# Which tiles are asked for when: three skipped loads and two halved scalings ahead of a mixture of experts

## The chip, the cores and the metric

The kernel runs on one core of a Trainium2 chip. The time is device time in microseconds (us), the median of three runs. TensorE (PE) multiplies; VectorE (DVE), ScalarE (ACT) and GpSimd (POOL) work on tiles in on-chip memory; SyncE (SP) issues nearly all direct transfers, in the order of its instruction queue, and POOL issues the indirect ones.

## What is computed

```python
# q, k, v: (8 batches, 8 heads, 576 positions, 64), float32
scores = q @ k.T / sqrt(64)
ret = scores * Dmat                  # gamma_h ** (i - j) for i >= j, else 0
x = (ret @ v) reshaped to (4608 tokens, 512)
g = argmax(x @ w_group)              # 4 groups, weight g_w = softmax
e = argmax(x @ w_expert[g])          # 4 experts in each, weight e_w = softmax
out[token] = g_w * e_w * (relu(x @ w1[g, e]) @ w2[g, e])      # w1 512x1024, w2 1024x512
```

## The kernel before

The program has two stages. The attention stage goes over 36 tiles of 128 tokens in one Python loop, `for t in range(NT + 1)`. The expert stage then goes over 16 experts, largest group first; the first expert's rows are cut in two passes, and the early one starts while the last attention tiles are still being finished.

Each attention tile has two inputs: `a` (queries and keys, 512 KB) and `b` (keys and values in another layout, 512 KB; every ninth tile needs only the values, 256 KB). They live in two rings of `RB = 7` buffers each, `r1` and `r2`. The weights of the experts use the same two rings: a piece `r` of `w1` (512 KB) takes a buffer of `r1`, a piece of `w2` (512 KB) one of `r2`. Four pieces of each make one expert.

Iteration t of the loop issues, on TensorE in this order: `av(t-1)` (masked scores times values, into `px`), `state(t)` (keys times scaled values, into `pst`), `inter(t-1)` (queries times the running state, into `px`), `scores(t+1)` (into `pss`), and then the transposes `pxt` and the small gate matmuls of earlier tiles. `scale(t+1)` stands ahead of them: it multiplies the values of the next tile by a factor for each head, as eight ScalarE instructions that read `b` and write `vs`. ScalarE then copies the state out of PSUM (`st<-pst`). On ScalarE the eight scalings of tile t+1 stand ahead of the copy of state t, and `state(t+1)` may not write `pst` before that copy has read it. VectorE masks the scores (`sT<-pss`) and scales the output (`xT<-px`). The order of the instructions on each engine is that of the program (a manual schedule on TensorE, `pin` on the others).

Loads run six tiles ahead: iteration t asks for tile t+6 (`loads(t + LOADS - 1, ...)`). From tile 8 on they are "paced": the DMA instruction also waits for the TensorE instruction just ahead of it in the program (`follow`). So in iteration 29 the last tile, 35, is asked for. The first expert is picked in iteration 28 (`pick(0)`, `expert_of(0)`: SP loads its number into a register). In iteration 29 its padding rows are written to the scratch tensor `xs` in DRAM, and `xload(0)` reads its 224 rows back as four transfers `xb`; on SP these wait until the scatters to `xs` that stand ahead of them have landed. The first expert's four weight pieces follow, one for `w1` and one for `w2` in each of the iterations 30 to 33 (`load_piece(r - 7)`). Weights of the second expert are asked for behind the loop.

Of the kernel before, what the change touches and what calls it, by code (L numbers as in the profile page):

```python
# [12 lines left out]
ALU = mybir.AluOpType  # L13
AX = mybir.AxisListType

P = 128
RG = 3
B, H, S, D = 8, 8, 576, 64
# [15 lines left out]
LOADS = 7  # L34
WARM = 8

FULL = 8
PACED = 8
NS = N + P
NT = N // P  # L40
NPIECE = 4
# [30 lines left out]
def moe_retention(ctx, tc, qk, kv, wgt, w1, w2, c_f, out):  # L72
# [7 lines left out]

    xs = dp.tile([E * NS, Q * WQ], F32, name="xs")

    cf = cp.tile([P, KC], F32, name="cf")
    gk = cf[:, KC_GK : KC_GK + 5 * H].rearrange("p (c h) -> p c h", c=5)
# [46 lines left out]
    dve, act, pool, sp = [Ordered(e_) for e_ in (nc.vector, nc.scalar, nc.gpsimd, nc.sync)]  # L131
# [3 lines left out]
    def follow(inst):  # L135

        tc.add_manual_dep(
            inst.ins, recent["pe"].ins.name,
            mybir.DependencyInfo(mybir.DependencyClass.Sync, mybir.DependencyReason.DATA),
            reason="loads apart in time",  # L140
        )
# [10 lines left out]
    def wload(e, pc, part):  # L152
        shape = [P, NKC, 2 * P] if part == 0 else [P, 2, DM]
        r = wp.tile(shape, F32, name=f"r{part + 1}_{e}_{pc}", tag=f"r{part + 1}", bufs=RB)
        w = (w1, w2)[part][bass.ds(ereg[e], 1), pc]
        sp.dma_start(r.rearrange("p c f -> p (c f)"), w.rearrange("o p x -> (o p) x"))
        return r
# [11 lines left out]
    def load_piece(i, parts=(0, 1)):  # L169
        if i < len(pieces):  # L170
            raws.setdefault(i, []).extend(wload(*pieces[i], part) for part in parts)
# [60 lines left out]
    def width_of(p):  # L232

        wide[p] = nc.values_load(
            sizes[0:1, p : p + 1], engines=[mybir.EngineType.PE], min_val=0, max_val=NS,
            skip_runtime_bounds_check_because="a count of rows, compared only",
# [46 lines left out]
    def xpad(p):  # L283

        apart("xs", pool.indirect_dma_start(
            out=xs, out_offset=bass.IndirectOffsetOnAxis(ap=pads[:, p % E : p % E + 1] if p else pad0, axis=0),
            in_=zero, in_offset=None, bounds_check=E * NS - 1, oob_is_err=False,
        ))
# [11 lines left out]
    def pad(rows, e, n, cap):  # L300

        pd = sm.tile([P, 2], F32, name=f"pd_{rows.name}", tag="pd")
        dve.tensor_scalar(pd[:, 0:1], sln[:, 0:1], n, None, ALU.add)
        dve.tensor_scalar(pd[:, 1:2], pd[:, 0:1], float(cap), float(E * NS), ALU.is_ge, ALU.mult)
        dve.tensor_tensor(pd[:, 0:1], pd[:, 0:1], pd[:, 1:2], ALU.add)
        dve.scalar_tensor_tensor(rows, e, float(NS), pd[:, 0:1], ALU.mult, ALU.add)

# [52 lines left out]
    tiles = []  # L360
    for bp in range(B // 2):
        for j in range(9):
            if j < 8:
                b, c = 2 * bp + j // 4, j % 4
# [79 lines left out]
    def xnat_store(t):  # L444
# [5 lines left out]
            out=xs, out_offset=bass.IndirectOffsetOnAxis(ap=g_["sl"][:, r : r + 1], axis=0),  # L450
            in_=xt.rearrange("p q w -> p (q w)"), in_offset=None, bounds_check=E * NS - 1, oob_is_err=False,
        ))
# [83 lines left out]
    def places_pe(t):  # L536

        n = RG
        ob = obs[-1]
        of = ob[:, 1:, :]  # L540
        pp = ps_sm.tile([P, n, E], F32, name=f"pp_{t}", tag="sm")

        def of_all(a):
            return a.unsqueeze(1).to_broadcast([P, n, E])

        pe.matmul(pp, up, of, start=True, stop=False)
        for r in range(1, n):
            pe.matmul(pp[:, r:, :], ones, ob[:, 1 : n - r + 1, :], start=False, stop=False)
        pe.matmul(pp, ones, of_all(ob[:, 0, :]), start=False, stop=False)
        pe.matmul(pp, ones, of_all(ensb), start=False, stop=True)  # L550
        tiles[t]["pp"] = pp
# [61 lines left out]
    def without():  # L613
        dve.tensor_scalar(mia[:, 0], slb, picked["c0"], float(BIG), ALU.is_ge, ALU.mult)
# [74 lines left out]
    with ExitStack() as ac:  # L689
# [7 lines left out]
        def loads(t, nms, paced=False):  # L697
            if t >= NT:
                return
            T = tiles[t]  # L700
            for nm in nms:

                T[nm] = wp.tile([P, 2, DM], F32, name=f"{nm}_{t}", tag=dict(a="r1", b="r2")[nm], bufs=RB)
                if T["m"] and nm == "b":
                    i_ = sp.dma_start(T[nm][:, 1], src[nm][t, :, 1])
                elif t:
                    i_ = sp.dma_start(T[nm], src[nm][t])
                if paced:
                    follow(i_)
            if t == 0 and nms == "b":  # L710

                for nm, i in (("b", 1), ("a", 0), ("a", 1), ("b", 0)):
                    sp.dma_start(T[nm][:, i], src[nm][t, :, i])
            if nms == "a":
                T["qT"], T["kT"] = [T["a"][:, i].rearrange("p (i j) -> p i j", i=NP) for i in range(2)]
            else:
                T["k"], T["v"] = [T["b"][:, i].rearrange("p (h d) -> p h d", h=H) for i in range(2)]
# [21 lines left out]
        def first_gq():  # L739

            dve.memset(gqs[0][:, :, 0:1], D**-0.5)
            for k in range(7):
                w = 2**k
                dve.tensor_tensor(
                    gqs[0][:, :, w : 2 * w], gqs[0][:, :, 0:w],
                    g2[:, :, k].unsqueeze(2).to_broadcast([P, 4, w]), ALU.mult,
                )
# [45 lines left out]
        def scale(t):  # L793

            T = tiles[t]
            T["vs"] = ap.tile([P, H, D], F32, name=f"vs_{t}", tag="vs", bufs=3)
            for h in range(H):
                act.activation(
                    T["vs"][:, h, :], T["v"][:, h, :], AF.Copy, scale=gk[:, T["c"], h : h + 1]
                )  # L800

        def scores(t):

# [111 lines left out]
        def group_end(t, lag):  # L915
            return t - lag + (t - lag + 1 == NT - RG - 1)

        scale(0)
        first_gq()
        scores(0)  # L920
        masked(0)
        for t in range(NT + 1):
            now = t < NT
            paced = t >= PACED
            if not paced:
                loads(t + LOADS - 1, "a")
            r = t - PICK

            choice = choose(group_end(t, 4)) if due(t, 4) else iter(())
            for _ in choice:  # L930
                if t >= NT - RG:
                    break
            if now and due(t, 5):
                places(group_end(t, 5))
            if r == 8:
                without()
            if t + 1 < NT:
                scale(t + 1)
            if t == NT:
                xnat_pe(NT - 6, ps_st)  # L940
            if t:
                av(t - 1)
            if t == NT - 1:
                second = pick(1)
                next(second)
            if not paced:
                loads(t + LOADS - 1, "b")
            if now:
                state(t)
            if paced:  # L950
                loads(t + LOADS - 1, "a", True)
            if t == NT:
                places_pe(NT - RG - 1)
            if t:
                inter(t - 1)
                if t == NT:
                    turned(t - 1)
                    places(NT - RG - 1)
                else:
                    turned(t - 1)  # L960
                    for _ in choice:
                        pass
            if r == 6:
                taken()
                close()
            if due(t, 4):
                weigh(group_end(t, 4))
            if t == NT - 1:
                next(second)
            if t + 1 < NT:  # L970
                scores(t + 1)
                masked(t + 1)
            late_consts(t)
            if now and 6 <= t:
                xnat_pe(t - 6)
                if paced:
                    loads(t + LOADS - 1, "b", True)
                xnat_out(t - 6)
            if now and due(t, 2):
                logits(group_end(t, 2))  # L980
            if due(t, 3):
                gate_pe(group_end(t, 3))
            if now and last_of_group(t - 4):
                places_pe(t - 4)

            u = t - 6
            while 0 <= u and "sl" in tiles[tiles[u]["grp"][-1]] and not tiles[u].get("out"):
                tiles[u]["out"] = True
                u -= 1
            for u in range(max(u + 1, 0), t - 5):  # L990
                if now:
                    xnat_store(u)
            if r == 5:
                for _ in pick(0):
                    pass
                expert_of(0)


            if r == 6:
                xload(0)  # L1000
            if 7 <= r <= 10:
                load_piece(r - 7)
            if r == 9:
                xturn(0, 0, 2)
                xturn(0, 1, 2)
                ids(0)
# [606 lines left out]
```

## Time and profile before

| | |
|---|---|
| median of 3 runs | 564.41 us (563.77 to 566.07) |
| profiled execution | 563.58 us, its span 561.8 us |
| TensorE busy | 547.5 us, 97% of the span |
| VectorE, ScalarE, GpSimd busy | 426.5, 328.0, 259.8 us |
| moved by DMA | 141.93 MB, mean 253 GB/s |
| granted TensorE clock | 0.999 of full speed |

The span runs from the first to the last instruction; the execution's own time is 1.8 us longer. The attention stage takes the first 142 us, and the expert stage the rest. A busy engine is not one at its peak, but with TensorE at 97% only gaps in its row, or work taken off it, can move the time by much. All times of the trace below are counted from the start of the span.

### The profile page before, as it was taken

The page shows a single profiled execution, that of the slowest core. Times are in us where ns is not written, and L with a number is a line of the kernel's source. Part 1 is how long each engine was busy: PE and PEld are TensorE (multiplying, and loading weights), DVE is VectorE, ACT ScalarE, POOL GpSimd, SP SyncE. Part 2 cuts the span into 40 slices and gives each one's busy share as a digit, 9 for nine tenths or more (in the row PEclk, how much of TensorE's full clock was granted, in tenths as well). Part 3 has the DMA queues.
Part 4 walks back from the last instruction along what each step waited for, and adds up shares of the span by engine and source line. Part 5 has one row for each costly group of instructions (what it writes and reads, how often), then busy time and mean ns, then how long its engine had stood idle before and what let it go on. Part 6 is the DMA issues. An engine that isn't in the chain of part 4 may idle for free. (4 is left out here: it accounts for less than half of the span.)

```text
span 561.8 us, 16944 instructions
## 1 busy us (share of the span) xinstructions
PE 547.5 (97%) x6137; PEld 522.7 (93%) x6137; DVE 426.5 (76%) x996; ACT 328.0 (58%) x855; POOL 259.8 (46%) x372
## 2 busy tenths in 40 slices
PE   7999989999999999999999999999999999999995
PEld 4888878878899999999999999999999999999995
DVE  5887768888789768976768596877778678787784
ACT  5687868877646545454555454555546555555554
POOL 0022423233504347464655628374665635638535
PEclk9999999999999999999999999999999999999999
DMA  8999999979784693847475674938475692865671
GB/s 329 416 414 338 342 357 326 371 269 367 268 264 178 179 345 89 324 115 286 128 282 167 244 242 164 325 112 329 120 281 185 239 341 73 331 193 208 227 287 47
DMA packets 61978, 141.93 MB, mean 253 GB/s; under 512 B 9164, under 2 KB 29780, under 8 KB 61872
## 3 DMA queue, kind: packets, MB, share of 16 engines
q1 hardware_dynamic: 52560, 120.32, 60.5%
q0 software_dynamic: 9168, 20.10, 9.4%
q8 instruction: 73, 1.20, 0.9%
q14 instruction: 33, 0.27, 0.1%
q10 hardware_dynamic: 144, 0.05, 0.0%
HBM read 120.08 MB, written 24.68 MB: 258 GB/s over the span
## 5 line engine op out<-in xcount | busy, mean ns | idle before, releaser
L125 POOL DMA_INDIRECT out<-y,ii x155 | 169.2, 1092 | 66.7 <-issue 30.9
L125 DVE TENSOR_TENSOR wl<-r,wh 128x512 fp32r<-128x512 f32 x268 | 172.2, 684 | 2.9
L125 ACT ACTIVATE hh<-ph 128x352 fp32r<-128x352 f32 (+16 forms) x128 | 53.6, 419 | 184.2 <-PE ph L651 136.5
L125 ACT CAST wh<-r 128x512 fp32r<-128x512 f32 x268 | 151.3, 618 | 0.0
L651 PE MATMUL ph<-xTh_m,wh 128*128 128x316 f32 (+12 forms) x504 | 147.2, 292 | 0.5 <-ACT xTh_m L125 0.5
L651 PE MATMUL ph<-xTl_m,wh 128*128 128x316 f32 (+12 forms) x504 | 146.9, 292 | 0.1
L651 PE MATMUL ph<-xTh_m,wl 128*128 128x316 f32 (+12 forms) x504 | 147.0, 292 | 0.0
L1103 PE MATMUL py<-hl,wh 128*128 128x316 f32 (+11 forms) x504 | 147.0, 292 | 0.0
L1101 PE MATMUL py<-hh,wh 128*128 128x316 f32 (+12 forms) x504 | 146.7, 291 | 0.0
L1102 PE MATMUL py<-hh,wl 128*128 128x316 f32 (+11 forms) x504 | 146.7, 291 | 0.0
L125 DVE SCALAR_TENSOR_TENSOR hl<-ph,hh 128x352 fp32r<-128x352 f32 (+15 forms) x126 | 58.2, 462 | 88.1 <-ACT hh L125 87.6
L651 PEld LDWEIGHTS ph<-xTh_m,wh 128*128 128x128 f32 x504 | 95.0, 189 | 0.6 <-ACT xTh_m L125 0.6
L651 PEld LDWEIGHTS ph<-xTl_m,wh 128*128 128x128 f32 x504 | 95.0, 188 | 0.4 <-DVE xTl_m L125 0.4
L1103 PEld LDWEIGHTS py<-hl,wh 128*128 128x128 f32 x504 | 95.0, 188 | 0.0
L651 PEld LDWEIGHTS ph<-xTh_m,wl 128*128 128x128 f32 x504 | 95.0, 189 | 0.0
L1102 PEld LDWEIGHTS py<-hh,wl 128*128 128x128 f32 x504 | 95.0, 188 | 0.0
L1101 PEld LDWEIGHTS py<-hh,wh 128*128 128x128 f32 x504 | 95.0, 188 | 0.0
L125 POOL COPY pace<-hh 1x1 f32<-1x1 f32 x118 | 29.9, 254 | 117.2 <-ACT hh L125 116.8
L125 POOL DMA_INDIRECT xs<-xt,sl x33 | 32.8, 995 | 96.9 <-DVE xT L125 39.5
L125 ACT ACTIVATE vs<-b,cf 128x64 f32<-128x64 f32 x288 | 72.4, 336 | 6.6 <-DMA b<-in_kv 5.5
L125 DVE TENSOR_TENSOR sT<-pss,masks 128x512 f32<-128x512 f32 x72 | 46.0, 680 | 10.1 <-PE pss L811 5.9
L867 PE MATMUL px<-sT,vs 128*64 128x128 f32 x576 | 39.4, 279 | 0.4 <-DVE xT L125 0.3
(187 smaller groups left out, 581.6 us busy)
## 6 DMA issues: line engine op xcount, KB each, us to landing
r<-in_w SPq DMA_DIRECT2D x138, 512.0 KB, 8.2
a<-in_qk SPq DMA_DIRECT2D x35, 512.0 KB, 6.2
b<-in_kv SPq DMA_DIRECT2D x31, 512.0 KB, 7.2
xb<-xs SPq DMA_DIRECT2D x20, 165.0 KB, 3.7
xb<-xs SPq DMA_DIRECT2D x20, 148.5 KB, 3.0
xb<-xs SPq DMA_DIRECT2D x16, 181.5 KB, 4.2
out<-y,ii POOLq DMA_INDIRECT x155, 3.4
b<-in_kv SPq DMA_DIRECT2D x6, 256.0 KB, 4.0
```

What stands on the lines that cost most here:

```text
L125: i_ = f(*a, **k)
L651: pe.matmul(ph[:, :wn], a[:, kc, cs], b[:, kc, x0 : x0 + wn], start=n == 0, stop=n == 3 * NKC - 1)
L867: recent["pe"] = pe.matmul(px[g * D : g * D + D, o, s * P : s * P + P], T["vs"][:, 4 * s + 2 * g + o, :], T["sT"][:, o, 2 * s + g, :], sta ...
L1101: pe.matmul(py[:, :w0], wh[:, f % 2, ds_], hh[:, :w0], start=st_, stop=False)
L1102: pe.matmul(py[:, :w], wl[:, f % 2, ds_], hh[:, :w], start=False, stop=False)
L1103: pe.matmul(py[:, :w], wh[:, f % 2, ds_], hl[:, :w], start=False, stop=sp_)
```

## The change

Three edits. First, iterations 12, 18 and 24 ask for no tile, and every later iteration asks for a nearer one: `ahead(t)` is t+6 up to tile 11, t+5 from 13, t+4 from 19 and t+3 from 25, so that tile 35 is asked for in iteration 32 and not 29. Second, the first expert's weight pieces come one iteration later and in halves, over the iterations 31 to 36. Third, for tiles 1 and 2 ScalarE scales four heads and VectorE the other four, in one instruction (`scale_rest`).

```diff
+SKIP = (12, 18, 24)
...
-            for h in range(H):
+            for h in range(H // 2 if t in (1, 2) else H):
...
+        def scale_rest(t):
+            T = tiles[t]
+            n = H // 2
+            dve.tensor_tensor(
+                T["vs"][:, n:], T["v"][:, n:],
+                gk[:, T["c"], n:].unsqueeze(2).to_broadcast([P, H - n, D]), ALU.mult,
+            )
...
+        def ahead(t):
+            return NT if t in SKIP else t + LOADS - 1 - sum(t > x_ for x_ in SKIP)
...
-                loads(t + LOADS - 1, "a", True)
+                loads(ahead(t), "a", True)
...
+            if t == 0:
+                scale_rest(1)
             if t:
                 inter(t - 1)
...
+            if t == 1:
+                scale_rest(2)
...
-                    loads(t + LOADS - 1, "b", True)
+                    loads(ahead(t), "b", True)
...
-            if 7 <= r <= 10:
-                load_piece(r - 7)
+            for i, part in {8: [(0, 0)], 9: [(1, 0)], 10: [(0, 1), (1, 1)], 11: [(2, 0), (2, 1)],
+                            12: [(3, 0)], 13: [(3, 1)]}.get(r, []):
+                load_piece(i, (part,))
```

No instruction is added to TensorE, POOL or SP, and their rows keep their order, except on SP. There the queue around iteration 29 read, before the change (`a_35` is the queries and keys of tile 35, `xb` the first expert's rows, `r1_0_0` the first piece of its `w1`, `r2_0_0` of its `w2`; `ISA` is register work; the repeated register loads and three more `xb` are left out):

```order
L125 DMA a_34_2415<-in_qk 128x1024
L125 DMA b_34_2443<-in_kv 128x1024
L250 TENSOR_LOAD e0i_71
...
L125 DMA a_35_2512<-in_qk 128x1024
L125 DMA b_35_2563<-in_kv 128x512
L125 ISA
L125 DMA xb_0_2575<-xs_63 32x7x132
...
L125 DMA r1_0_0_2673<-in_w1 128x1024
L125 ISA
L125 DMA r2_0_0_2675<-in_w2 128x1024
```

And after the change:

```order
L126 DMA b_32_2545<-in_kv 128x1024
L126 ISA
L126 DMA xb_0_2557<-xs_63 32x7x132
...
L126 DMA a_33_2604<-in_qk 128x1024
L126 DMA b_33_2648<-in_kv 128x1024
L126 DMA a_34_2695<-in_qk 128x1024
L126 DMA b_34_2731<-in_kv 128x1024
L126 ISA
L126 DMA r1_0_0_2749<-in_w1 128x1024
L126 DMA a_35_2779<-in_qk 128x1024
L126 DMA b_35_2806<-in_kv 128x512
L126 ISA
L126 DMA r1_0_1_2819<-in_w1 128x1024
```

The inputs of tiles 33, 34 and 35, which stood ahead of the four `xb` transfers, now stand behind them, and behind the wait that the first of these has.

On VectorE the start of the program gains two instructions, each between the masked scores of one tile and of the next (after the change):

```order
L126 TENSOR_TENSOR sT_0_195<-pss_110,masks_114 128x512 x2
L126 TENSOR_TENSOR vs_1_200<-b_1_140,cf_64 128x256
L126 TENSOR_TENSOR sT_1_227<-pss_110,masks_114 128x512 x2
L126 TENSOR_TENSOR xT_0_258<-px_0_237,gq0_115 128x4x128
L126 TENSOR_TENSOR vs_2_232<-b_2_144,cf_64 128x256
L126 TENSOR_TENSOR sT_2_269<-pss_110,masks_114 128x512 x2
```

Before, the two rows with `vs` were not there, and ScalarE's queue held eight scalings for each of these tiles where it now holds four.

## Rows read from the trace of the kernel before

**Rows 1.** The page's first part: busy time, share of the span, instructions.

```profile
PE 547.5 (97%) x6137; PEld 522.7 (93%) x6137; DVE 426.5 (76%) x996; ACT 328.0 (58%) x855; POOL 259.8 (46%) x372
```

**Rows 2.** Timeline of TensorE, 40 to 82: start, time, instruction, idle before it.

```profile
43.90 0.34 PE L852 MATMUL pst<-vs,b 128*64 128x64 f32 x4 [1.18 <-issue]
...
71.60 0.49 PE L412 MATMUL pxt<-cf,xT 128*128 128x128 f32 x3 [0.76 <-issue]
...
77.91 0.69 PE L852 MATMUL pst<-vs,b 128*64 128x64 f32 x16 [0.98 <-ACT xt L125]
```

**Rows 3.** Timeline of TensorE at the start, same columns.

```profile
11.32 0.69 PE L852 MATMUL pst<-vs,b 128*64 128x64 f32 x16 [0.66 <-ACT st L125]
...
19.39 1.09 PE L867 MATMUL px<-sT,vs 128*64 128x128 f32 x16
20.31 0.64 PE L852 MATMUL pst<-vs,b 128*64 128x64 f32 x16
```

**Rows 4.** Timeline of ScalarE at the start.

```profile
9.00 2.02 ACT L125 ACTIVATE vs<-b,cf 128x64 f32<-128x64 f32 x8 [3.25 <-DMA b<-in_kv]
10.92 0.35 ACT L125 COPY st<-pst 128x256 f32<-128x256 f32 x1
11.51 2.02 ACT L125 ACTIVATE vs<-b,cf 128x64 f32<-128x64 f32 x8 [0.24 <-DMA b<-in_kv]
...
17.88 2.02 ACT L125 ACTIVATE vs<-b,cf 128x64 f32<-128x64 f32 x8 [1.50 <-DMA b<-in_kv]
19.81 0.35 ACT L125 COPY st<-pst 128x256 f32<-128x256 f32 x1
```

**Rows 5.** Timeline of VectorE at the start.

```profile
9.69 1.29 DVE L125 TENSOR_TENSOR sT<-pss,masks 128x512 f32<-128x512 f32 x2 [1.26 <-PE pss L811]
...
23.89 0.75 DVE L125 TENSOR_TENSOR gq<-gq,cf 128x256 f32<-128x256 f32 x2
```

**Rows 6.** Timeline of SP's queue: issue start, time, transfer.

```profile
105.60 0.33 SPq L125 DMA_DIRECT2D b<-in_kv  x1
...
117.16 0.33 SPq L125 DMA_DIRECT2D b<-in_kv  x1
122.39 1.92 SPq L125 DMA_DIRECT2D xb<-xs  x4
124.57 19.28 SPq L125 DMA_DIRECT2D r<-in_w  x11
```

**Rows 7.** Timeline of GpSimd's queue, the last scatter ahead of `xb`.

```profile
119.00 0.99 POOL L125 DMA_INDIRECT xs<-xt,sl  x1 [0.28 <-POOL xt L125]
```

**Rows 8.** DMA of SP's queue, 122 to 128.1: packets, MB, share of 16 engines.

```profile
q1 hardware_dynamic: 1100, 1.00, 69.5%
```

**Rows 9.** The same, 122 to 129.9.

```profile
q1 hardware_dynamic: 1240, 1.51, 71.5%
```

**Rows 10.** Timeline of TensorE around tiles 29 and 33.

```profile
114.18 0.64 PE L852 MATMUL pst<-vs,b 128*64 128x64 f32 x16
...
127.28 0.90 PE L823 MATMUL pss<-a 64*64 64x128 f32 x32
...
129.02 1.09 PE L867 MATMUL px<-sT,vs 128*64 128x128 f32 x16
129.94 0.63 PE L852 MATMUL pst<-vs,b 128*64 128x64 f32 x16
...
134.30 0.64 PE L852 MATMUL pst<-vs,b 128*64 128x64 f32 x16
```

**Rows 11.** Transfers by line, 0 to 200: count, KB each, median us to landing.

```profile
b<-in_kv SPq DMA_DIRECT2D x31, 512.0 KB, 7.2
...
xb<-xs SPq DMA_DIRECT2D x4, 115.5 KB, 2.3
```

**Rows 12.** DMA of the instruction queue in 75 to 75.5.

```profile
q8 instruction: 1, 0.02, 17.9%
```

**Rows 13.** The weight pieces issued in 124 to 132: times to landing.

```profile
DMA to landing us min/median/max: 9.1/9.4/9.7
```

## What was predicted

> **What bounds the kernel now.** I began with the busy times. TensorE is busy for 547.5 of 561.8 us [rows 1], and no other engine comes near that, so the time can move in three ways: a gap on TensorE goes, a gap comes, or work is taken off it. The change takes no work off it. So I looked for TensorE's gaps, in its timeline. From about 20 us to 110 us the attention stage has three, of 1.18, 0.76 and 0.98 us [rows 2], in iterations 10, 17 and 19. In two of them nothing that the profile shows was waited for ("issue"), and in the third an output copy of ScalarE is named, which that matmul does not read. At the very start, before 20 us, there is a gap of 0.66 us in which `state(1)` waits for ScalarE [rows 3]. ScalarE itself waits there for data: 3.25 us for the values of tile 1 and 1.50 us for those of tile 4 [rows 4]. From 20 us on no gap of TensorE is put down to a load. Loads are early now, and the question is whether they still are after the change.
>
> **Part one, two scalings on two engines.** For tile 1, ScalarE starts its eight scalings at 9.00 us, and the copy of state 0 behind them starts at 10.92 [rows 4], 1.92 us later; with four scalings it starts some 0.96 us earlier. VectorE's half is one instruction over 256 elements. Two of this size with the same kind of broadcast factor took 0.75 us [rows 5], so one takes some 0.37 us. It lies in VectorE's wait of 1.26 us ahead of the masked scores at 9.69 [rows 5], since the data come at 9.00. That cover gone, it would cost up to 0.37 us. So `state(1)` starts at least its 0.66 us of waiting earlier, and tile 2, whose values come at 11.51 [rows 4], keeps this because it is split as well. It does not last. The values of tile 4 arrive at 17.88, the copy behind their eight scalings starts at 19.81 and takes 0.35 us [rows 4], so `state(4)` cannot start before 20.16. It started at 20.31, straight behind the matmuls of 19.39 [rows 3]. At most 0.15 us is left of the gain. When tile 4 arrives is set by the transfers ahead of it, which the change doesn't touch. The bounds are -0.66 us (if tile 4 came earlier too) and +0.37; I take -0.10.
>
> **Part two, the tiles that are asked for later.** The order of SP's queue decides. The inputs of tiles 33 and 34 now stand behind the four `xb` transfers. The first `xb` waits for scatters, the last of which POOL issued at 119.00 [rows 7]; SP issued its last tile load at 117.16 and then nothing until 122.39, and the four took it 1.92 us [rows 6]. So `a_33` is issued at about 124.3 and `b_33` at about 124.8, where the first weight pieces were issued at 124.57 [rows 6]. These pieces have the size of a tile's input, so they show what happens to a transfer at this place. From 122 to 128.1 SP's queue moved 1.00 MB [rows 8]; the four `xb` of 115.5 KB [rows 11] are 0.47 of that, which leaves 0.53 MB, one input of 512 KB (0.52 MB). By 129.9 it had moved 1.51 MB [rows 9], that is 1.04 MB without `xb`, two inputs. If transfers of this queue end in the order of issue, `a_33` is there at 128.1 and `b_33` at 129.9.
>
> TensorE wants `a_33` at 127.28 for `scores(33)` [rows 10], 0.8 us too early. Then `state(33)`, which ran at 129.94 [rows 10], needs the copy behind eight scalings of `b_33`: 129.9 + 1.92 + 0.35 [rows 4] is 132.2. That is 2.3 us late, with the 0.8 inside it. Queued behind it on TensorE is all the rest of the attention stage, and on ScalarE the state copy and the rows' output of the tile; the scatters wait for these in turn. Tile 34 adds nothing: at 0.51 MB in 1.8 us its values are there by about 133.7, the copy behind their scalings ends at 136.0, and `state(34)`, 134.30 [rows 10] and 2.3 later, comes at 136.6. Nothing gives the 2.3 us back, as TensorE is busy from there on. Bounds: +0.8 (only `a_33` is late) and +6.2 (rival three). I take +2.3.
>
> [...]
>
> The other loads have a shorter lead too. The tightest is `b_29`: issued in iteration 26, where the `b` of 105.60 was [rows 6], and wanted 2.27 us ahead of `state(29)` at 114.18 [rows 10], which is 6.3 us later. The median landing is 7.2 us over all `b` of 512 KB [rows 11], the flood of the start included. After three iterations without a load the queue is 3 MB shorter, so I cost this at nothing; at 7.2 us it would be 0.9 us. The weight pieces cost nothing: the first is issued within some 3 us of 124.57, and with the 9.7 us that pieces took there [rows 13] it lands while tile 35 is still being worked on.
>
> **Part three, what the thinner queue gives back.** Of the three gaps, the last ends at 77.91 [rows 2], and a packet of the instruction queue began at 75 to 75.5 [rows 12]; such a single packet stands between 2 and 3 us ahead of the end of each of the three. I read them as TensorE out of instructions, because the packet came late among data. The gap at 43.90 lies before iteration 12 and stays. That at 77.91 follows directly on iteration 18, which asks for nothing now; that at 71.60 is five iterations behind the one at 12. The bounds are -1.74 (both go) and +1.18 (a new one of the largest size). I take the nearest, -0.98.
>
> [...]
>
> **Sum.** The profiled execution took 563.58 us by itself, its span 561.8. With -0.10, +2.3 and -0.98 it becomes 564.80. The median of the runs is 0.83 above the profiled execution, and I carry that over: 565.6, which is 1.2 us or 0.2% above 564.41. A measurement of this kernel can tell about 0.5% from no change, which is 2.8 us: below 561.6 is faster, above 567.2 slower.
>
> **Rivals.** One: tile 33 is nearly hidden and the queue's relief is full. An `xb` landed in 2.3 us [rows 11]; the 0.41 MB by which an input is larger take 1.4 us at 0.51 MB in 1.8 us. Then `b_33` lands 3.7 us behind 124.8, at 128.5, and `state(33)` is 0.9 late; both gaps go. 563.58 - 0.10 + 0.9 - 1.74 + 0.83 gives 563.5. For it: the queue is emptier when SP comes to `a_33`. Against it: it was just as empty before `xb` in the present trace.
>
> Two: the change doesn't do what it says. Tile 33's wait is made good by a shorter queue ahead of `xb`, and the instruction gaps only move. Only part one is left: 564.3. For it: SP's wait is for a scatter, which a thinner queue lets land earlier. Against it: 2.3 us would have to come out of the 3.4 us from 119.00 to 122.39 [rows 6, 7].
>
> Three, on the slower side: transfers that are in flight together share the queue and land together. The pieces issued at 124 to 132 landed after 9.1 to 9.7 us [rows 13]. With 9.1, `b_33` lands at 133.9, `state(33)` is possible at 136.2, 6.2 us late, and the time is 563.58 - 0.10 + 6.2 - 0.98 + 0.83, which is 569.5. It decides from the point where `b_33` lands after about 131.5, since the 3.9 us then lost put the time above 567.2. For it: those landings. Against it: at the start the values of tiles 1, 2 and 4 came at 9.00, 11.51 and 17.88 [rows 4], one tile after the other and not together.
>
> **How the numbers follow.** The forecast gets 50%, rival one 25%, two 12%, three 13%. The forecast's own range, with tile 33 from 1.5 to 3.2 us and the gaps from -1.74 to 0, is 564.1 to 567.5. The range for 8 in 10 reaches down into rival one, to 563.0, and ends at 567.8, which leaves out most of rival three. Faster by over 0.5% needs rival one and the gap at 43.90 as well: 5%. Slower by over 0.5% is rival three and the upper end of the forecast: 17%. Within 0.5% is the rest, 78%.
>
> **What would show it.** In the profile after: `state(1)` without a wait, and ScalarE waiting for tile 4 longer than 1.50 us. SP issuing `a` and `b` right behind `xb`, and ScalarE's scalings of tile 33 waiting for `b`, with a gap of 2 to 3 us ahead of `pst` near 130 on TensorE. At most two "issue" gaps in the attention stage. I am wrong if no such wait stands near 130, if it is above 4 us, or if loads end waits in iterations 25 to 29.

## The result: 0.6% slower, and the profile after

The kernel after takes 568.6 us (median of 7 runs, 566.42 to 571.0). The kernel before took 564.41 beside it (7 runs, 563.65 to 566.07). The ratio is 1.006, with a 95% interval of 1.0036 to 1.0085. That is 3.0 us above the 565.6 of the forecast and 0.8 above the end of its range of 8 in 10 (by the ratio, 1.006 times 564.41, it is 567.8, the end itself). By the bound of 0.5% the middle of the interval lies on the slower side, and the forecast had given most of its chance to no difference. The direction and the place were right. The size was not.

The profiled execution took 568.60 us, with a span of 566.5, so it stands for the median. TensorE's busy time, the page's first part, hardly moved against [rows 1]:

```profile
PE 549.2 (97%) x6137; PEld 524.2 (93%) x6137; DVE 427.1 (75%) x998; ACT 326.4 (58%) x847; POOL 260.1 (46%) x372
```

So a wait was added. TensorE's timeline from tile 32 to the first expert has it, beside [rows 10]:

```profile
126.51 0.63 PE L862 MATMUL pst<-vs,b 128*64 128x64 f32 x16
...
130.56 0.90 PE L833 MATMUL pss<-a 64*64 64x128 f32 x32 [3.41 <-DMA a<-in_qk]
...
134.83 0.69 PE L862 MATMUL pst<-vs,b 128*64 128x64 f32 x16 [1.43 <-ACT st L126]
...
139.23 0.63 PE L862 MATMUL pst<-vs,b 128*64 128x64 f32 x16
...
147.32 1.02 PE L676 MATMUL ph<-xTf,r 128*128 128x224 f32 x4 [0.26 <-DVE xT L126]
```

The first row is `state(32)`, 0.2 us earlier than the 126.71 of before. `scores(33)` waits 3.41 us for `a_33`, and `state(33)` another 1.43, and it stands at 134.83 where it stood at 129.94: 4.89 us late. ScalarE's timeline names what the second wait is for, `b_33`:

```profile
132.50 2.02 ACT L126 ACTIVATE vs<-b,cf 128x64 f32<-128x64 f32 x8 [6.30 <-DMA b<-in_kv]
134.43 0.35 ACT L126 COPY st<-pst 128x256 f32<-128x256 f32 x1
```

The next tile adds nothing (134.83 to 139.23 is 4.4 us, before 4.36), and the first expert's matmul is 4.42 later than the 142.90 of before. The span is 4.7 longer. So one place holds nearly the whole loss: from `state(32)` to `state(33)` it is 8.32 us where it was 3.23, 5.09 more; 0.2 had been gained ahead of it, and 0.5 comes back between `state(34)` and the first expert. SP's queue, beside [rows 6], and the last scatter on GpSimd's, beside [rows 7], show the order that the prediction had expected:

```profile
116.91 0.33 SPq L126 DMA_DIRECT2D b<-in_kv  x1
123.20 2.02 SPq L126 DMA_DIRECT2D xb<-xs  x4
125.32 0.39 SPq L126 DMA_DIRECT2D a<-in_qk  x1
125.81 0.37 SPq L126 DMA_DIRECT2D b<-in_kv  x1
126.28 0.41 SPq L126 DMA_DIRECT2D a<-in_qk  x1
```

```profile
118.81 1.00 POOL L126 DMA_INDIRECT xs<-xt,sl  x1 [0.28 <-POOL xt L126]
```

Elsewhere little changed. Of the three gaps of [rows 2], the one at 71.60 has gone, and two have stayed:

```profile
44.51 0.34 PE L862 MATMUL pst<-vs,b 128*64 128x64 f32 x4 [1.47 <-issue]
...
77.54 0.69 PE L862 MATMUL pst<-vs,b 128*64 128x64 f32 x16 [0.93 <-ACT xt L126]
```

At the start, beside [rows 3, 4], `state(1)` no longer waits, but the first 16 matmuls of the scores take 2.08 us where they took 1.16, so it starts no earlier (11.39, before 11.32), and `state(4)` comes at 20.58 where it came at 20.31:

```profile
5.81 2.08 PE L821 MATMUL pss<-a 64*128 64x128 f32 x16 [1.17 <-DMA a<-in_qk]
...
11.39 0.64 PE L862 MATMUL pst<-vs,b 128*64 128x64 f32 x16
...
20.58 0.69 PE L862 MATMUL pst<-vs,b 128*64 128x64 f32 x16
```

```profile
18.25 2.02 ACT L126 ACTIVATE vs<-b,cf 128x64 f32<-128x64 f32 x8 [2.07 <-DVE gq L126]
20.17 0.35 ACT L126 COPY st<-pst 128x256 f32<-128x256 f32 x1
```

### The profile page after: what moved, and what is told of

Read it like the earlier page. It is cut to its first block, busy times and chain, and to the rows that moved or that the text cites. A ratio compares the mean times of both kernels' runs of the same rounds, so it can differ in the third digit from the quotient of the medians.

```text
span 566.5 us, 16934 instructions
## 1 busy us (share of the span) xinstructions
PE 549.2 (97%) x6137; PEld 524.2 (93%) x6137; DVE 427.1 (75%) x998; ACT 326.4 (58%) x847; POOL 260.1 (46%) x372
## 5 line engine op out<-in xcount | busy, mean ns | idle before, releaser
L126 ACT ACTIVATE vs<-b,cf 128x64 f32<-128x64 f32 x280 | 70.6, 335 | 16.9 <-DMA b<-in_kv 14.7
```

The source lines that it names most:

```text
L126: i_ = f(*a, **k)
```

## The experiments

The theory: tile 33 is late because its inputs stand behind `xb` and its wait in SP's order. Its rivals: the bytes in flight at that point make some transfer late whatever the order; or the time is lost at the start, where two tiles' values are split.

The runs were made on several chips. On the two chips of e1 to e11 the kernel before took 588.19 to 594.94 us (medians). Each ratio is to runs of the kernel before on the same chip, and times of different groups are not compared. Intervals between starts of the same matmuls in the attention stage's last part can be: for each run, taken from its TensorE timeline, the start of `state(32)`, and the time from it to `state(33)`, from there to `state(34)`, from there to the first expert matmul, and the sum, all in us.

| run | ratio, 95% | state(32) | to 33 | to 34 | to expert | sum |
|---|---|---|---|---|---|---|
| before | 1 | 126.71 | 3.23 | 4.36 | 8.60 | 16.2 |
| after | 1.006 (1.0036 to 1.0085) | 126.51 | 8.32 | 4.40 | 8.09 | 20.8 |
| before again (e10) | 1.0015 (0.9982 to 1.0048) | 132.98 | 3.54 | 4.79 | 8.88 | 17.2 |
| split alone (e3) | 0.9993 (0.9955 to 1.0031) | 129.84 | 3.58 | 4.81 | 8.87 | 17.3 |
| no tile skipped (e2) | 1.0034 (1.0001 to 1.0067) | 130.75 | 3.55 | 4.79 | 8.88 | 17.2 |
| constants later (e8) | 1.005 (1.0004 to 1.0096) | 131.52 | 3.52 | 4.85 | 8.90 | 17.3 |
| two tiles skipped (e5) | 1.0032 (0.9991 to 1.0074) | 131.86 | 3.53 | 4.84 | 8.93 | 17.3 |
| after again (e6) | 1.0122 (1.0060 to 1.0185) | 129.96 | 6.92 | 4.94 | 9.47 | 21.3 |
| xb behind tile 33 (e1) | 1.0073 (1.0043 to 1.0103) | 131.65 | 4.86 | 5.85 | 9.18 | 19.9 |
| xb behind all (e7) | 1.0101 (1.0043 to 1.0158) | 131.34 | 3.51 | 4.82 | 11.30 | 19.6 |
| tile 34 held back (e4) | not timed | 131.13 | 7.11 | 4.98 | 11.97 | 24.1 |
| xb on GpSimd (e9) | 1.0139 (1.0057 to 1.0220) | 131.11 | 3.90 | 10.13 | 9.89 | 23.9 |
| the same, none skipped (e11) | 1.0107 (1.0067 to 1.0148) | 130.83 | 4.61 | 9.35 | 10.23 | 24.2 |
| e9, transposes later (e12) | 1.0032 (1.0009 to 1.0056) | 129.12 | 3.22 | 7.81 | 9.79 | 20.8 |

Before, after and e12 ran where the kernel before takes 564 to 565 us, so their base is 16.2. For the others it is 17.2 to 17.3.

**Parts of the change alone.** e3 is the kernel before with the split of the two early tiles' scalings; e2 is the kernel after with `SKIP = ()`, that is with the split and the weights in halves; e5 asks for no tile twice.

```diff
-SKIP = (12, 18, 24)
+SKIP = ()            # e2
+SKIP = (12, 18)      # e5
```

> The kernel before with the scalings of tiles 1 and 2 split over ScalarE and VectorE, and nothing else. Prediction's part one: 0.10 us faster than before, at most 0.7, so 563.7 to 564.5, with state(4) held at about 20.2 to 20.6 us by the values of tile 4. Rival (the start of the program got worse in the changed kernel, where 16 matmuls took 2.08 in place of 1.16 us): state(4) later than 20.31 and a time 0.3 to 1 us above before.

> The changed kernel without the three skipped loads (SKIP empty): the split scalings and the halved, later weight pieces alone. Theory A: nothing of a tile stands behind xb, so the time is that of before within 1 us, 563.5 to 565.5. Rival C: the loss is in these two parts, and the time is 567 to 569.

> The changed kernel with two skipped loads (12 and 18) in place of three, so that the last tiles are asked for four ahead: tile 33 stands ahead of xb on SP, tiles 34 and 35 behind it, with one tile more of time. Theory A (the loss is the data of tiles 33 and 34 coming late because three ahead is too short where the xb transfers and the wait ahead of them fall): no wait on TensorE for tile 33, none or under 0.5 us for tile 34, and 3 to 5 us less than the changed kernel on the same chip. Rival B (skipping costs by itself, at the start or in the middle): within 1.5 us of the changed kernel.

None of the three has a wait at tile 33: their sums are those of the kernel before again (e10). e5 takes 596.32 us where the kernel after takes 600.33 on the same chip (e6). So the loss needs the third skipped tile, which leaves a lead of three tiles and puts `a_33` and `b_33` behind `xb`. With e5's lead of four tiles they still stand ahead of it. (The ratio of e2 lies a little above 1 all the same, 1.0001 to 1.0067. What makes that is not shown.) In e3, TensorE's and ScalarE's timelines show why the split gives nothing. `state(1)` runs at 10.69, 0.63 us earlier than before, but the values of tile 4 arrive when they do:

```profile
18.42 2.02 ACT L126 ACTIVATE vs<-b,cf 128x64 f32<-128x64 f32 x8 [1.75 <-DMA b<-in_kv]
20.35 0.35 ACT L126 COPY st<-pst 128x256 f32<-128x256 f32 x1
```

```profile
10.69 0.69 PE L862 MATMUL pst<-vs,b 128*64 128x64 f32 x16 [0.21 <-ACT st L126]
...
20.75 0.69 PE L862 MATMUL pst<-vs,b 128*64 128x64 f32 x16 [0.62 <-ACT st L126]
```

`state(4)` waits 0.62 us for the copy behind them. In e8, the transfers of two constants were moved from behind tile 3's loads to behind tile 5's, so that tile 4 might come earlier:

```diff
-                if t == 3:
+                if t == 5:
                     sp.dma_start(wgp, ...)
```

> The kernel before with the split scalings of tiles 1 and 2 and with the two transfers of constants (64 and 106 KB) issued behind tile 5's inputs in place of tile 3's. It tests what holds the gain of part one: if the arrival of tile 4 does, its values come some 0.4 to 1.2 us earlier, state(4) runs at about 19.6 to 20.0 in place of 20.31, and the time falls by 0.3 to 0.7 us, too little for the interval but visible in the trace. Rival: state(4) stays at 20.2 to 20.8, since the data of tile 4 are not what holds it.

It gained nothing either (1.005, 1.0004 to 1.0096). Tile 4 did come earlier: ScalarE starts its scalings at 16.59 without a wait for data, where in e3 it waited for them until 18.42.

```profile
16.59 2.02 ACT L126 ACTIVATE vs<-b,cf 128x64 f32<-128x64 f32 x8
```

But the first two groups of scores took 2.08 us each here, TensorE and not tile 4 set the pace, and `state(4)` ran at 21.99. So what the earlier tile is worth can't be read from e8.

**The place of xb.** e1 issues `xb` one iteration later (`if r == 7`), behind `a_33` and `b_33`. e7 issues it behind all attention inputs, and its transposes two iterations later.

```diff
-            if r == 6:
-                xload(0)
+                    if r == 9:       # e7, behind loads(ahead(t), "b", True)
+                        xload(0)
-            if r == 9:
+            if r == 11:
                 xturn(0, 0, 2)
```

> The changed kernel with one edit: the first expert's rows xb are asked for at the end of iteration 30 in place of 29, so that the inputs of tile 33 stand ahead of them on SP. Theory A (tile 33 starves behind xb, 4.9 us in the trace of the changed kernel): a_33 and b_33 are there before 125, the waits of 3.4 and 1.4 us on TensorE at tile 33 go, tile 34 still comes in time, xb itself is issued when it was, and the time falls by 4 to 5 us to 563 to 564.5. Rival B (the shorter lead of the loads costs in many places, and tile 33 only collects it): another wait takes over and the time stays above 567. Rival C (the split scalings or the halved pieces cost it): no change, 568.

> The changed kernel with xb behind the inputs of all tiles: asked for in iteration 32 just behind b_35, and turned in iteration 34. Three skips stay. Theory A: the data of tiles 33, 34 and 35 come in time (b_33 within 6 us of its issue, no small xb packets beside it), TensorE's waits at tiles 33 and 34 are under 0.5 us together, and the time is 3 to 5 us under the changed kernel. If three tiles of lead are too short even without xb, waits of 1 to 3 us stay at tiles 28 to 34.

e1 was to give back 4 to 5 us and gave back about a third of the loss by the table: its sum is 2.7 above the base, in place of 4.1 in e6. Its ratio can't be told from that of e6, as the intervals overlap. ScalarE still waits, for `b_33`, issued 126.58 just ahead of `xb`, and for `b_34`, issued 130.08 behind it:

```profile
134.18 2.02 ACT L126 ACTIVATE vs<-b,cf 128x64 f32<-128x64 f32 x8 [2.84 <-DMA b<-in_kv]
...
140.04 2.02 ACT L126 ACTIVATE vs<-b,cf 128x64 f32<-128x64 f32 x8 [1.10 <-DMA b<-in_kv]
```

ScalarE starts on them 7.6 and 10 us after their issue, and VectorE waits 1.93 us for `xb`, which stands between them. In e7 TensorE waits for no tile at all (3.51 and 4.82 are the base), but now `xb`, issued at 139.17, is late. The median is 598.38 us, 2.0 under e6, where 3 to 5 were expected. VectorE transposes `xb` at 144.30, and TensorE's next work queued behind that:

```profile
144.30 1.17 DVE L126 STREAM_TRANSPOSE xTf<-xb 128x384 f32<-128x384 f32 x2 [1.44 <-DMA xb<-xs]
```

```profile
147.28 1.51 PE L877 MATMUL px<-sT,vs 128*64 128x128 f32 x16 [2.24 <-DVE xT L126]
```

So the order theory is right about who waits, and it is not the whole story: what went second was late (ScalarE waits 1.10 us for `b_34` in e1, VectorE 1.44 for `xb` in e7).

**Landing times.** e4 holds the inputs of tile 34 back until `scores(33)` runs, and the first weights behind them, so that only `a_33` and `b_33` are in flight behind `xb`.

```diff
+                if t in (32, 33):
+                    loads(t + 2, "a", True)
+                    loads(t + 2, "b", True)
```

> The changed kernel, but the inputs of tiles 34 and 35 are asked for only when TensorE has done the scores of the tile before, and the first expert's weight pieces start in iteration 33: behind xb only a_33 and b_33 are in flight. If transfers of SP's queue end in the order of issue, a_33 lands as late as in the changed kernel, 5.1 us behind its issue, and b_33 6.7. If those in flight share the queue, a_33 lands about 3.5 us and b_33 about 4.7 us behind the issue. The time itself will be worse, 569 to 575, as tile 34 then starves too.

Its two transfers were issued at 129.75 and 130.38, and TensorE and ScalarE start on them at:

```profile
134.23 0.90 PE L833 MATMUL pss<-a 64*64 64x128 f32 x32 [2.47 <-DMA a<-in_qk]
```

```profile
135.91 2.02 ACT L126 ACTIVATE vs<-b,cf 128x64 f32<-128x64 f32 x8 [4.95 <-DMA b<-in_kv]
```

That is 4.5 and 5.5 us, between the two expectations, and no less than in e6, where the inputs of tile 34 are in flight behind them (4.3 and 5.4). So sharing with later transfers is not shown by this pair. When the queue had moved the bytes is in the DMA view of e4 from 127.6 on, to 133.5 and to 135:

```profile
q1 hardware_dynamic: 1097, 1.01, 65.2%
```

```profile
q1 hardware_dynamic: 1242, 1.51, 70.2%
```

`xb` with `a_33` is 0.99 MB, with `b_33` as well 1.51. If the bytes are counted in the order of issue, a consumer starts 0.7 to 0.9 us behind the byte count, even where nothing follows. e6, with everything in flight behind, shows the same 0.7 and 0.75 (0.98 MB at 132.0 and start at 132.71; 1.51 MB at 133.8 and start at 134.55).

**The changed kernel and the kernel before, again.** e6 is the kernel after and e10 the kernel before, each unchanged on another chip.

> The changed kernel itself, on the chip of this group, as the mark for the other three. Theory A: 3 to 5 us above before on this chip, with the same waits at tile 33 (3.4 and 1.4 us in its first trace). Rival B: the same time, but from waits that stand elsewhere on this chip.

> The kernel before, unchanged, for its trace on the chip of the other runs here. If the three gaps of TensorE of 1.18, 0.76 and 0.98 us belong to the kernel's instruction blocks among its loads, they stand at the same places, 43.9, 71.6 and 77.9; if they belong to one execution or one chip, other places and sizes, and the sum of TensorE's gaps between 30 and 118 us is some 1.6 us as in the runs with and without the skipped tiles. state(1) waits 0.66 us for ScalarE, and state(4) starts within 0.3 us of 20.75, the start with the scalings split; by the rival (the split shortens the start) at 21.2 or later. Ratio 1.000.

In e6, TensorE waits 2.12 us for `a_33`, `state(33)` is 3.4 us late by the table, and then something else shows.

```profile
132.71 0.90 PE L833 MATMUL pss<-a 64*64 64x128 f32 x32 [2.12 <-DMA a<-in_qk]
...
134.78 1.98 PE L877 MATMUL px<-sT,vs 128*64 128x128 f32 x16
136.88 0.93 PE L862 MATMUL pst<-vs,b 128*64 128x64 f32 x16
```

The 16 matmuls ahead of `state(33)` take 1.98 us, where they took 1.09 in [rows 10], and fill the time in which it would have waited for the state copy (136.48 to 136.83 on ScalarE). In the view by stretch (us; time and count of PE, PEld, DVE, ACT, POOL; granted clock; DMA share; GB/s) the clock falls to 0.50 of full speed behind the wait:

```profile
133.00:135.00 2.00, 2.00 (x41) 1.60 (x34) 1.31 (x3) 0.45 (x2) 0.00 (x0) 0.76 1.04 420
135.00:137.00 2.00, 1.88 (x18) 1.48 (x18) 1.86 (x6) 2.00 (x9) 0.00 (x0) 0.50 1.02 413
137.00:139.00 2.00, 2.00 (x64) 1.87 (x64) 0.22 (x1) 0.76 (x3) 0.81 (x1) 0.88 1.02 410
```

In the first profile after it read 1.00 from 130 to 138, with the longer wait of 3.41 us there.

e10 helps with two points. The gaps of [rows 2] are not in every execution of the kernel: in e10 none of 0.5 us or more stands at 43.9, 71.6 or 77.9, and one of 1.22 us stands at 109.73, in the middle of a group of equal matmuls:

```profile
107.79 0.72 PE L823 MATMUL pss<-a 64*64 64x128 f32 x21
109.73 0.55 PE L823 MATMUL pss<-a 64*64 64x128 f32 x11 [1.22 <-issue]
```

But they do not fall anywhere either. The gap at 43.90 stands behind the 12th of the 16 matmuls of the state in iteration 10. Behind the same 12th matmul there is one of 1.47 us in the profile after, one of 2.02 in e12 (below), and this in e2, which skips no tile:

```profile
44.92 0.34 PE L862 MATMUL pst<-vs,b 128*64 128x64 f32 x4 [0.58 <-issue]
```

The other ten profiles have none of 0.5 us or more there. So the place comes back, and the size is open from one execution to the next.

And the slow first scores are not of the change, since e10 has them, in its first two groups, and e6, the changed code, has not (with them e10's `state(1)` does not wait and `state(4)` runs at 22.00, so it is no mark for the start):

```profile
5.40 2.08 PE L811 MATMUL pss<-a 64*128 64x128 f32 x16 [0.75 <-DMA a<-in_qk]
```

```profile
5.79 1.16 PE L821 MATMUL pss<-a 64*128 64x128 f32 x16 [1.23 <-DMA a<-in_qk]
```

**xb past SP.** e9 is the kernel after with `xb` issued from GpSimd's queue (which loads the expert's number as well), so that SP's loads wait for no scatter; e11 is the same with `SKIP = ()`.

```diff
-            i_ = sp.dma_start(
+            i_ = (sp if p else pool).dma_start(
```

> The changed kernel with one thing moved: the four xb transfers are issued from GpSimd's queue and not from SP's, behind the same scatters. SP then comes to the inputs of tiles 33 and 34 without standing behind xb's wait, some 3 to 5 us earlier than in the changed kernel. Theory A (the place behind xb's wait in SP's order is what makes tile 33 late): no load ends a wait of TensorE above 0.5 us at tiles 33 and 34, and the ratio to the kernel before is 0.997 to 1.004. Theory B (the bytes of xb, and loads that land together, make it late, wherever SP stands): the inputs still land 8 to 10 us behind their issue, TensorE waits 1 to 2.5 us at tile 33 or 34, and the ratio is 1.005 to 1.010. Theory C (xb itself comes late from GpSimd's queue): a gap of 1 us or more ahead of the first expert, ended by xT.

> As the first of these, xb from GpSimd's queue, but no tile without a load. It says what the move of xb costs by itself. Theory A: no wait for a load at tiles 33 and 34, ratio 0.997 to 1.004, the same as with the skipped tiles. If the shorter queue of the skipped tiles were worth anything (the part of the change that was to give time back), the run with them would be 0.5 us or more ahead of this one at the first expert matmul; by the rival they differ by less.

Theory A was right that no load ends a wait at tile 33 (3.90, with a 0.20 "issue" gap in it), and wrong on the time (1.0139). `xb` itself is late now, as theory C had it, at another place than expected. GpSimd issues the four transfers from 128.70 to 130.6, VectorE can start on them at 138.96, 8.4 us behind the last issue, and TensorE stands behind VectorE:

```profile
138.96 1.17 DVE L126 STREAM_TRANSPOSE xTf<-xb 128x384 f32<-128x384 f32 x2 [3.06 <-DMA xb<-xs]
```

```profile
141.66 1.51 PE L459 MATMUL plt<-xT,wgp 128*32 128x384 f32 x8 [3.73 <-DVE xT L126]
```

e11 does the same without skipped tiles (24.2 against 23.9), so no gain from the skipped tiles shows where the order doesn't hurt them. e12 then moves e9's transposes two iterations later (`if r == 11`):

> The changed kernel with xb issued from GpSimd's queue, and with VectorE's transposes of xb (with the row numbers read from it) two iterations later, where the run before had VectorE wait 3.06 us for xb and TensorE 3.73 behind it. Theory A (every us lost by the change is somebody waiting for whichever transfer was put last behind the scatters: the inputs of tile 33 if xb goes first, xb if the inputs go first; a consumer that comes late enough waits for neither): no wait of TensorE above 0.5 us from 125 to 148 us, first expert matmul at 149 to 150.5, with a wait of about 1 us as in the kernel before, ratio 0.998 to 1.004. If the three tiles without a load gave something back, the ratio would be below 0.998. Theory B (the load on the DMA engines is the limit at that point, whatever the order): a wait of 1.5 us or more comes up elsewhere, at the loads of tiles 33 to 35, at xb, or at the first weights, and the first expert matmul stays at 151.5 or later, ratio 1.006 to 1.012.

No load and no `xb` stops TensorE for more than 0.5 us now, as theory A had it, but the sum is 20.8 and not 16.2. TensorE waits 0.97 us for VectorE, which has the transposes in its way at 144.21, and 2.45 us for nothing that the timeline shows, the second of these rows (the first is the gap of iteration 10, ahead of what the sum covers):

```profile
45.24 0.34 PE L862 MATMUL pst<-vs,b 128*64 128x64 f32 x4 [2.02 <-issue]
...
138.21 0.18 PE L549 MATMUL pp<-ob,ones 128*128 128x16 bf16 x1 [2.45 <-issue]
```

Behind the second gap the clock is at 0.58 and 0.57 of full speed in the stretches from 138 to 140 and to 142. This profiled execution took 570.29 us, the longest of its ten (median 567.52), so how much of this is in the others is not shown. The ratio, 1.0032 (1.0009 to 1.0056), lies in theory A's range and under the 1.006 of the kernel after, but the two intervals overlap, and theory A wanted no wait above 0.5 us. The run does not settle whether it is the load on the DMA engines that costs the rest. No version tried beats the kernel before.

## Why the prediction was off, step by step

**What bounds the kernel** held: the time moved by TensorE's gaps, and by one above all.

**Part one** (-0.10 us) held in mechanism, as e3 shows: `state(1)` 0.63 us earlier, and tile 4 takes the gain back. In the profile after, `state(1)` waits no more, and ScalarE is idle longer ahead of tile 4 (2.07 us in place of 1.50). The +0.27 us measured at `state(4)` goes with tile 4's scalings starting at 18.25 and not 17.88. The profile puts that wait down to `gq` of VectorE, where e3 has it at the data, so what came last there is open. First scores of either length occur with and without the split.

**Part two** is where it failed, in size: `state(33)` was forecast 2.3 us late, at 132.2, and was 4.89 late, at 134.83. (Counted from `state(32)`, tile 33 cost 5.09.) The order and the waiting engines were right, and the missing recovery but for 0.5 us. Its two sentences on time were not. "`a_33` is issued at about 124.3": it was 125.32, 1.0 later. The scatter was issued 0.2 us earlier than before, yet SP was held 0.8 us longer, and the four `xb` took 0.1 longer to issue. This is more than one execution: from the issue of the last scatter to that of the first `xb` it is 4.39 us here, 4.15 in e6 and 4.33 in e4, the kernels with three skipped tiles and `xb` in its place, and 3.1 to 3.6 before and in e2, e3, e5, e8 and e10. Why is open. The thinner queue did not let `xb` go earlier, which is against what rival two hoped for. And "if transfers of this queue end in the order of issue, `a_33` is there at 128.1 and `b_33` at 129.9" took the moment at which the queue had moved the bytes for the moment at which a consumer can start. In the kernel after, from 123 to 129.3 and to 131, the DMA view has

```profile
q1 hardware_dynamic: 1092, 0.98, 62.0%
```

```profile
q1 hardware_dynamic: 1232, 1.49, 69.1%
```

so, counted in the order of issue, the bytes of `b_33` were through at about 131.1, 5.3 us behind its issue, where the forecast had 5.1. ScalarE started at 132.50, 1.4 us later. 1.0 of the issue, 0.2 of the bytes and 1.4 behind them make 2.6, which is 4.89 less 2.3. Of the 1.4, some 0.7 to 0.9 stand in e4 and e6 too. What the rest is on the first chip stays open. Rival three, all transfers landing together after 9.1 us, was too pessimistic for `a_33` and `b_33`, on which TensorE and ScalarE started 5.2 and 6.7 us behind the issue, though `b_34` took 9.4 us. The prediction's own mark, a wait above 4 us, was reached with 3.41 and 1.43.

The loads with a shorter lead cost nothing, as forecast: iterations 25 to 29 have no such wait on TensorE, and `state(32)` is 0.2 us early. The room was nearly used up, though: ScalarE waits 0.52 us for `b_29` at 110.88 and 0.37 for `b_30` at 114.47, 5.5 and 5.4 us behind their issue, where the prediction had counted 6.3 us of room.

**Part three** (-0.98 us) failed as a reading. By `state(32)` the kernel after was 0.2 us ahead, some 0.5 with the start's 0.27 taken out, and by another gap than the one named: the one behind the skipped iteration 18 stayed, with 0.93 us, and the one at 71.60 went. The gap of iteration 10 stayed, as the prediction had it. e10 has no large gap at these places, and e9 and e11 reach `state(32)` at 131.11 and 130.83 with and without skipped tiles. The sizes change with the execution, and a term for them belonged in the range and not in the sum. What the gaps are is not shown, and that TensorE was out of instructions there was the author's reading. A packet of the instruction queue stands 2 to 3.2 us ahead of their end, after the change as in [rows 12], in e10 in 107 to 107.5, and in e12 in 135 to 135.5. But from 41 to 81 us the trace before has eight such packets and three such gaps, so most packets have none behind them, and no run changed the packets alone.

**Sum.** To the 563.58 us come 0.27 at the start, -0.47 by the gaps up to `state(32)`, 5.09 at tile 33, and -0.47 from there to the first expert's matmul, which makes 568.0. Measured were 568.60; another 0.3 came in the rest of the expert stage and 0.3 outside the span, and nothing here shows why. Of the forecast's terms, -0.10 was 0.27, 2.3 was 5.09, and -0.98 was -0.47. A range that went up only to 3.2 us for tile 33, while bounds of +0.8 and +6.2 were worked out, was too narrow.

## What to carry to other kernels

When a change shortens how far ahead loads are asked for, look for the next instruction on the issuing queue that waits for something else, and count which loads fall behind it. That gives the place of the loss; for its size, take landing times of transfers issued under the same load, as TensorE and ScalarE started here 0.7 to 1.4 us after the queue had moved the bytes. A gap without a releaser in one profile is no stock to draw on: the same gap, at the same instruction, was 2.02 us in one profile here, 0.58 in another, and not there in most, so it takes several profiles to price it.

## What the runs showed of the hardware that was not expected

- The first 16 score matmuls take 1.16 us in some executions and 2.08 in others of the same code (before 1.16 and e10 2.08, after 2.08 and e6 1.16). From 4 to 8 us the granted clock was 1.00 both before and after.
- With some waits of TensorE the granted clock fell. It was 0.50 in e6 from 135 to 137, behind a wait of 2.12 us, in e9 from 140 to 146, where a wait of 3.73 ended at 141.66, and in e11 from 144 to 146, behind one of 3.56; in the first profile after it was 1.00 from 130 to 138, with the wait of 3.41. The four transposes `pxt` next behind the wait took 1.11 us in e7 (a wait of 2.24) and 0.66 in e4 (2.47) and in the first profile after. In e6 this cost little, as `state(33)` had to wait anyway (to `state(34)` 4.94 us, in e10 4.79). In e9 that stretch is 5.3 us longer than in e10, of which the wait is 3.73. e9, from 140 on:

```profile
140.00:142.00 2.00, 0.34 (x4) 0.20 (x8) 1.88 (x8) 0.97 (x5) 0.33 (x2) 0.50 1.05 423
142.00:144.00 2.00, 2.00 (x19) 0.84 (x13) 1.81 (x9) 1.85 (x7) 0.00 (x0) 0.50 1.02 408
144.00:146.00 2.00, 2.00 (x30) 2.00 (x26) 1.07 (x4) 2.00 (x9) 0.25 (x1) 0.50 1.02 412
```

- The four small `xb` transfers, 2.3 us to landing when they go first [rows 11], were waited for until 8.4 us behind the last issue when they went out from GpSimd, with inputs of 512 KB already issued from SP (e9).
